# A dilated convolution with a gate: one more family of products split into shared and private parts, and the gate's product moved from VectorE to GpSimd

## The chip, the cores and the metric

The kernel runs on one core of a Trainium2 chip. The metric is the device time of one execution in microseconds (us). PE is TensorE (PEld its weight loads), DVE is VectorE, ACT is ScalarE, POOL is GpSimd, SP is SyncE, which here only issues DMAs.

## The reference

```python
B, T, D, K = 2, 16000, 144, 15          # x: (B,T,D), w: (K,D,2D), w_o: (D,D), all bfloat16
dil = 2; pad = (K - 1) * dil
xp = jnp.pad(x, ((0, 0), (pad, 0), (0, 0)))
h = sum(einsum('btc,cd->btd', xp[:, pad - i*dil : pad - i*dil + T, :], w[i]) for i in range(K))
z = tanh(h[..., :D]) * sigmoid(h[..., D:])
return z @ w_o
```

It is a causal convolution in time with 15 taps and dilation 2 from 144 to 288 channels, a gate (tanh of one half times sigmoid of the other), and a 144 x 144 projection.

## The kernel before, in words

**Tiling.** Time is cut into 16 windows of 2048 steps (8 for each of the two sequences). A window is loaded transposed (`xn`: 128 channels on partitions, time along the free dimension). The other 16 channels go another way: `xt` is gathered, ACT and DVE turn it into two signals `xs` (steps `cr` and `dr`), these are written to a DRAM buffer `xg` (`wg`) and come back transposed as `rx` and `re`, in which 8 taps x 16 channels fill the 128 partitions. A window has two octets, one for each parity `rho` of time, since the dilation is 2; there are 32 octets. An octet is 128 x 8 outputs of 288 channels: partition m and phase r stand for time 16 m + 2 r + rho. The output of a phase is accumulated in a PSUM bank of 128 x 288 fp32.

**Fewer products.** The 15 taps (and a zero one, `w_all`) are applied by a nested fast scheme: DVE forms differences of the signal in time (`d2`, `d4`, `d8`, `d24`, `d28`, `d48`, `d248`: the name lists the shifts), sums of taps are formed once, and sums that several outputs share are computed once. The class `Leaf` is a product with a shared and two private parts: `common` (two matmuls into a first bank; step `v`), `copy` (ACT copies that bank into a second one; step `k`), `private(i)` (two matmuls into bank i, and a third on `rx` or `re` where the leaf has a remainder; step `p`). `dup` (step `d`) has ACT copy a bank once more. The leaves are A1, A2, A3 (two banks of the pool `ps_a`) and B1, C1, E1 (five banks of the pool `ps_bc`). A method `direct` adds products with single taps into a bank without sharing: B2 and B3 for the even phases, C2 for the odd ones (five matmuls each, for i = 0 and 1).

**From banks to outputs.** ACT copies A1 to SBUF (`a1s`). DVE forms q2 = a1s - A2 and q3 = a1s + A3, and from them and the banks the fp32 outputs `y[:, k + 4 i, :]`: yB2 (k = 0), yC2 (k = 1), yB3 (k = 2), yC3 (k = 3). For yC3 a `t3` = q3 + C1 comes first and E1 is added; for yC2 the C1 bank holds C1 and C2 together. Gate 0 (k = 0 and 2, steps `th0`, `sg0`) and gate 1 (k = 1 and 3, `th1`, `sg1`) are each one tanh and one sigmoid of 576 elements on ACT; `m0` and `m1` are their products z, on DVE. A DMA transposes z (`zt`), eleven matmuls in three groups project it (`g0` to `g2`), ACT casts the result (`po0` to `po2`), and the second octet of a window stores it (`ost`).

**Order.** All engines are scheduled by hand: an engine runs its instructions in program order, and waits on other engines by semaphores; buffers of a pool are given out in rotation. The program order comes from the list `PLAN`: each entry `name:at` says that octet n's step is issued in period n + at, at its place in the list. The list is cyclic: one pass is one period, that is one octet's worth of every engine's work. Steps that belong to a window (the loads, the remainder, the differences) are issued for even n alone. The list `first` issues the beginning of octet 0, and `finish_early` and `finish` the end: the last octet's z is transposed on PE, and the last three octets are projected there.

Of the kernel before, what the change touches and what calls it, by code (L numbers as in the profile page):

```python
# [26 lines left out]
def kernel(  # L27
# [14 lines left out]
    nc = tc.nc  # L42
# [88 lines left out]
    pad = {"x": 0, "d8": 0}  # L131

    def derive_steps(s):
        ahead = {"x": 0}

        def sub(name, of, d, first=None, run=0):
# [4 lines left out]
            def go(which=slice(None)):  # L141
# [15 lines left out]
                for form in forms[which]:  # L157
# [6 lines left out]
                    d28=sub("d28", "d2", 8, 6, 4), d24=sub("d24", "d2", 4, 2, 4), d248=sub("d248", "d24", 8, 8, 2))  # L164
# [97 lines left out]
    ev = wtile(2, "ev")  # L262
# [82 lines left out]
    class Octet:  # L345
        by_phase = False

        def __init__(self, s, rho):
            self.s, self.rho = s, rho
            self.A1 = Leaf(s, True, "x", "d8", rho, lambda j: a1v[:, j, :], lambda j, i: ss[:, 2 * j + i, :])  # L350
            self.A2 = Leaf(s, s is not sets[0] or rho > 0, "d4", "d48", rho - 4, lambda j: av[:, j, 1, :], lambda j, i: quad[:, j, i, 1, :],
                           ("rx", rho, ns_r[:]))
            self.A3 = Leaf(s, True, "d4", "d48", rho, lambda j: av[:, j, 0, :], lambda j, i: quad[:, j, i, 0, :],
                           ("rx", rho + 4, s_r[:]))
            self.B1, self.C1 = (Leaf(s, False, "d2", "d28", rho - 2 * e, lambda j, e=e: bcv[:, j, e, :],
                                     lambda j, i, e=e: bc[:, 2 * j + i, e, :]) for e in (1, 0))
            self.E1 = Leaf(s, False, "d24", "d248", rho, lambda j: ev[:, j, :], lambda j, i: w_all[:, 8 * j + 4 * i, :], ("re", rho + 4, we_r[:]))
            self.g, self.t, self.po = {}, {}, {}

        def get(self, pool, name, shape, dt):  # L360
            if name not in self.t:
                self.t[name] = pool.tile(shape, dt, name=name)
            return self.t[name]
# [19 lines left out]
        def C2(self, i):  # L383
            self.direct(self.C1.ts[i], self.rho - 4 + 8 * i, lambda j: w_all[:, 4 * j + 2, :], 4, "re", self.rho + 8 * i, we_r[:])

        def t3(self, i):
            nc.vector.tensor_tensor(out=self.get(cp_pool, "t3", [P, 2, D2], F32)[:, i, :], in0=self.t["q3"][:, i, :],  # L387
                                    in1=self.C1.ts[i][:, 0:D2], op=ALU.add)

        def out_y(self, k, ts, q, op, i):  # L390
            y = self.get(y_pool, "y", [P, 8, D2], F32)
            nc.vector.tensor_tensor(out=y[:, k + 4 * i, :], in0=self.t[q][:, i, :], in1=ts[i][:, 0:D2], op=op)  # L392

        def act(self, k, name, lo, func):
            t = act_pool.tile([P, 4, D], BF16, name=name)
            self.g[name, k] = t
            nc.scalar.activation(out=t[:], in_=self.t["y"][:, k::2, lo:lo + D], func=func)  # L397

        def mult(self, k, part):
            z = self.get(z_pool, "z", [P, 9, CM], BF16)  # L400
            o, lo, n = dict(a=(z[:, k:8:2, :], 0, CM), b=(z[:, 8, :].rearrange("p (r c) -> p r c", c=CR)[:, k::2, :], CM, CR),
                            z=(z[:].rearrange("p g c -> p (g c)").rearrange("p (r c) -> p r c", c=D)[:, k::2, :], 0, D))[part]
            th, sg = self.g["th", k], self.g["sg", k]
            nc.vector.tensor_tensor(out=o, in0=th[:, :, lo:lo + n], in1=sg[:, :, lo:lo + n], op=ALU.mult)  # L404
# [6 lines left out]
    def z_by_pe(o, blocks, by):  # L411

        zt, z = o.get(zt_pool, "zt", [P, 9, P], BF16), o.t["z"]
        for i in range(0, len(blocks), 4):
            b = blocks[i:i + 4]
            ps = bank(True)[:].bitcast(BF16).rearrange("p (g m) -> p g m", m=256)
            for k, g in enumerate(b):
                nc.tensor.transpose(ps[:, k, 0:P], z[:, g, :], ident[:])
            copy_by(by, zt[:, b[0]:b[-1] + 1:2, :], ps[:, 0:len(b), 0:P])
        o.zt = zt  # L420
# [7 lines left out]
    def outproj(o, g, end=False):  # L428
        r0, n = 3 * g, min(3, 8 - 3 * g)
        o.po[g] = bank(False) if end else ps_o.tile([P, 512], F32, name="po", tag="po")  # L430
        if not o.by_phase:
            for c in range(r0, r0 + n + 1):
                a, e = max(c - 1, r0), min(c + 1, r0 + n)
                nc.tensor.matmul(o.po[g][:, (a - r0) * D:(e - r0) * D], lhsT=o.zt[:, c, :],  # L434
                                 rhs=wo_z[:, c, a - c + 1:e - c + 1, :].rearrange("p r e -> p (r e)"), start=c == r0, stop=c == r0 + n,
                                 skip_group_check=True)
            return
        nc.tensor.matmul(o.po[g][:, 0:n * D], lhsT=o.zt[:, 8, :], rhs=wo_bd[:, r0:r0 + n, :].rearrange("p r e -> p (r e)"),  # L438
                         start=True, stop=False)
        for i in range(n):  # L440
            nc.tensor.matmul(o.po[g][:, i * D:(i + 1) * D], lhsT=o.zt[:, r0 + i, :], rhs=wo_m[:], start=False, stop=i == n - 1)  # L441
# [16 lines left out]
    def issue(n, name):  # L458
# [16 lines left out]
        if name[0] in "vkpd" and name[1] in "ABCE":  # L475
# [7 lines left out]
        elif name[:2] == "t3":  # L483
            o.t3(int(name[-1]))
        elif name[:3] == "a1s":
            o.a1s(int(name[-1]))
        elif name[0] == "q":
            o.q(*((o.A2, "q2") if name[1] == "2" else (o.A3, "q3")), int(name[-1]),
                ALU.subtract if name[1] == "2" else ALU.add)
        elif name[0] in "BC":  # L490
            getattr(o, name[0:2])(int(name[-1]))
        elif name[0] == "y":
            leaf = {"B": o.B1, "C": o.C1, "E": o.E1}["E" if name[1:3] == "C3" else name[1]]
            ts, q = (leaf.other, "q3") if name[1:3] == "B3" else (leaf.ts, "t3" if name[1:3] == "C3" else "q2")
            k = (0 if name[1] == "B" else 1) + (2 if name[2] == "3" else 0)
            o.out_y(k, ts, q, ALU.subtract if name[1] == "B" else ALU.add, int(name[-1]))
        elif name[:2] == "th":
            o.act(int(name[2]), "th", 0, ACT.Tanh)
        elif name[:2] == "sg":
            o.act(int(name[2]), "sg", D, ACT.Sigmoid)  # L500
        elif name[0] == "m":
            for part in "ab" if o.by_phase else "z":
                o.mult(int(name[1]), part)
        elif name == "zt":
            o.zt = z_load(o.t["z"])
# [14 lines left out]
    def finish_early():  # L520

        n = NO - 3
        for g in range(3):
            outproj(live[n], g, g > 0)
        for g, by in ((0, "DVE"), (1, "DVE"), (2, "ACT")):
            project_out(live[n], window_out(n), g, by)
        z_by_pe(live[NO - 1], [0, 2, 4, 6], "ACT")

    def finish():
        n = NO - 2  # L530
        store(NW - 2, nc.sync)
# [17 lines left out]
    at_wg = next((at, i) for i, (name, at) in enumerate(plan) if name == "wg")  # L549
    def weights_out():  # L550
# [4 lines left out]
        nc.gpsimd.tensor_copy(out=held[:], in_=ev[0:1, 0, 0:1])  # L555
# [9 lines left out]
    def evs():  # L565
        add(ev[:], w_all[:, 0:16:8, :], w_all[:, 4:16:8, :])
        weights_out()
# [9 lines left out]
    done = [(0, f) for f in first if not callable(f)] + late2 + [(0, "d24"), (0, "d248")]  # L577
    todo = sorted((2 + at_wg[0], False, at_wg[1] - .5, n, name) if n == 2 and name in ("cr", "dr") else
                  (n + at, n > 1 and n + at < 0, i, n, name) for i, (name, at) in enumerate(plan) for n in range(NO)
                  if not (name in even and (n % 2 or n == 0) or name == "ost" and n % 2 == 0  # L580
                          or name in outwards and n >= NO - 3 or name == "zt" and n == NO - 1))
    gates = [(NO - 1, "m1")]
    for *_, n, name in todo:
        if (n, name) in done:
            continue
        if (n, name) in gates:
            gates.clear()
            finish_early()
        issue(n, name)
    finish()  # L590
# [28 lines left out]
```

## Time and profile before

| what | value |
|---|---|
| time, median of 3 runs | 332.19 us (331.83 to 332.69) |
| the profiled execution: its own time | 332.82 us |
| its span, instructions | 330.8 us, 7432 |
| PE busy, matmuls | 321.4 us (97%), 2657 |
| DVE busy, instructions | 293.5 us (89%), 664 |
| ACT busy, instructions | 242.0 us (73%), 571 |
| POOL busy, instructions | 26.3 us (8%), 56 |
| granted TensorE clock, mean | 0.999 |

The profile is of one execution, so numbers from it are made against 332.82 us; 2.0 us of that lie outside the span. A duration is from an instruction's start to its end; instructions of one engine overlap a little, so that the distance of two starts is what an instruction takes from its engine. Matmuls are pipelined: a busy PE isn't PE at its peak, and for them too the distance of starts counts. After an arrow the profile names who ended the idle time before an instruction.

### The profile page before, as it was taken

How to read it: one execution, taken by the hardware profiler on the slowest of the kernel's cores; microseconds unless marked ns; L12 is line 12 of the kernel's file. 1: busy time of each engine (PE TensorE's matmuls, PEld its weight loads, DVE VectorE, ACT ScalarE, POOL GpSimd, SP SyncE). 2: the span in 40 equal slices, each digit the busy share in tenths (PEclk: the TensorE clock that was granted, in tenths of full speed). 3: DMA queues.
4: the chain of work that ended last, by engine and by line, in shares of the span. 5: the costliest groups of instructions: out<-in, count | busy, mean ns of one | idle time of the engine just before them, and what ended most of it. 6: DMA issues, size and time to landing. Idle time of an engine off the chain costs nothing.

```text
span 330.8 us, 7432 instructions
## 1 busy us (share of the span) xinstructions
PE 321.4 (97%) x2657; PEld 303.1 (92%) x2657; DVE 293.5 (89%) x664; ACT 242.0 (73%) x571; POOL 26.3 (8%) x56
## 2 busy tenths in 40 slices
PE   8899999999999999999999999999999999999993
PEld 3589999999999999999999999999999999999982
DVE  2889999989999998999999899999989999998683
ACT  2737777777877777788777778877777787777763
POOL 5959100000000000000000000000000000000000
PEclk9999999999999999999999999999999999999999
DMA  8779897895949579594979769495986859594113
GB/s 173 160 139 157 155 210 138 151 185 100 206 109 204 151 130 222 77 213 102 175 181 169 157 119 187 109 209 137 145 208 119 171 112 189 154 143 132 38 36 129
DMA packets 194993, 49.64 MB, mean 150 GB/s; under 512 B 190487, under 2 KB 192896, under 8 KB 194957
## 3 DMA queue, kind: packets, MB, share of 16 engines
q1 hardware_dynamic: 188894, 40.07, 69.6%
q10 hardware_dynamic: 4799, 8.58, 7.0%
q0 software_dynamic: 1264, 0.53, 0.9%
q8 instruction: 20, 0.33, 0.4%
q14 instruction: 16, 0.13, 0.1%
HBM read 2.82 MB, written 11.40 MB: 43 GB/s over the span
## 4 chain that ended last, share of the span: by engine, by line
PE 90%; DMA 4%; SPq 2%; DVE 2%; issue 1%; POOL 1%; ACT 0%; DVEq 0%
PE bc L302 56%; PE a L302 25%; PE po L434 9%; DMA xn<-in_x_dram 2%; DMA xt<-in_x_dram 1%; SPq L128 1%; DMA xg<-zero 1%; SPq L89 1%; DVE d L160 0%; DVE o L426 0%; DVE y L392 0%; DVE z L404 0%; POOL xg L123 0%; PE bc L438 0%; PE bc L441 0%
## 5 line engine op out<-in xcount | busy, mean ns | idle before, releaser
L302 PEld LDWEIGHTS <-d 128*128 128x128 bf16 x1792 | 225.4, 145 | 7.8 <-issue 1.4
L302 PE MATMUL bc<-w_all,d 128*128 128x288 bf16 x832 | 140.0, 286 | 0.3 <-DVE t L387 0.3
L392 DVE TENSOR_TENSOR y<-q,bc 128x288 f32<-128x288 f32 x192 | 86.4, 450 | 7.6 <-PE bc L302 5.7
L331 ACT COPY bc<-bc 128x288 f32<-128x288 f32 x97 | 38.5, 397 | 30.1 <-PE bc L302 24.3
L369 DVE TENSOR_TENSOR q<-a1s,a 128x288 f32<-128x288 f32 x126 | 54.2, 451 | 1.5 <-PE a L302 0.8
L424 ACT CAST o<-po 128x432 bf16<-128x432 f32 (+1 forms) x87 | 41.7, 479 | 17.1 <-PE po L434 17.1
L160 DVE TENSOR_TENSOR d<-d 128x516 bf16<-128x516 bf16 (+3 forms) x65 | 52.2, 805 | 0.0
L302 PE MATMUL a<-sm,d 128*128 128x288 bf16 x252 | 50.2, 286 | 0.0
L331 ACT COPY a<-a 128x288 f32<-128x288 f32 x95 | 36.6, 386 | 13.6 <-PE a L302 10.6
L160 DVE TENSOR_TENSOR d<-xn 128x516 bf16<-128x516 bf16 (+2 forms) x48 | 41.1, 859 | 5.1 <-DMA xn<-in_x_dram 5.1
L397 ACT ACTIVATE th<-y 128x576 bf16<-128x576 f32 x64 | 43.9, 685 | 1.1 <-DVE y L392 1.1
L397 ACT ACTIVATE sg<-y 128x576 bf16<-128x576 f32 x64 | 43.7, 683 | 0.0
L434 PE MATMUL po<-wo_z,zt 128*128 128x144 bf16 (+1 forms) x323 | 43.4, 253 | 0.0
L302 PE MATMUL bc<-bc,d 128*128 128x288 bf16 x256 | 41.8, 286 | 0.0
L302 PE MATMUL bc<-wo_p,re 128*128 128x288 bf16 x128 | 36.6, 286 | 0.0
L302 PE MATMUL bc<-we_r,re 128*128 128x288 bf16 x128 | 36.6, 286 | 0.0
L387 DVE TENSOR_TENSOR t<-q,bc 128x288 f32<-128x288 f32 x64 | 28.8, 451 | 8.3 <-PE bc L302 8.3
L434 PEld LDWEIGHTS <-zt 128*128 128x128 bf16 x341 | 29.9, 98 | 4.1
L335 ACT COPY bc<-bc 128x288 f32<-128x288 f32 x64 | 25.0, 393 | 11.2 <-PE bc L302 7.0
L392 DVE TENSOR_TENSOR y<-t,bc 128x288 f32<-128x288 f32 x64 | 26.1, 450 | 5.9 <-PE bc L302 5.9
L404 DVE TENSOR_TENSOR z<-th,sg 128x576 bf16<-128x576 bf16 (+1 forms) x66 | 29.1, 443 | 0.0
L302 PEld LDWEIGHTS <-re 128*128 128x128 bf16 x256 | 28.8, 113 | 0.0
(79 smaller groups left out, 275.5 us busy)
## 6 DMA issues: line engine op xcount, KB each, us to landing
out_dram<-o ACTq DMA_DIRECT2D x13, 576.0 KB
xg<-xs SPq DMA_DIRECT2D x30, 65.0 KB
xt<-in_x_dram SPq DMA_DIRECT2D x13, 71.5 KB
w_all<-in_w_dram SPq DMA_DIRECT2D x3, 288.0 KB
out_dram<-o SPq DMA_DIRECT2D x1, 576.0 KB
zt<-z SPq DMA_TRANSPOSE x31
out_dram<-o ACTq DMA_DIRECT2D x1, 468.0 KB
out_dram<-o ACTq DMA_DIRECT2D x1, 288.0 KB
```

The source lines that it names most:

```text
L89: nc.sync.dma_start_transpose(out=xn[:, lo:WB], in_=src)
L160: nc.vector.tensor_tensor(out=o, in0=a, in1=b_, op=ALU.subtract)
L302: nc.tensor.matmul(ps[:, 0:D2], lhsT=l, rhs=r, start=start, stop=stop, skip_group_check=on)
L331: nc.scalar.copy(out=self.ts[1][:, 0:D2], in_=self.ts[0][:, 0:D2])
L335: nc.scalar.copy(out=self.other[i][:, 0:D2], in_=self.ts[i][:, 0:D2])
L369: nc.vector.tensor_tensor(out=self.get(cp_pool, name, [P, 2, D2], F32)[:, i, :], in0=self.t["a1s"][:, i, :], in1=leaf.ts[i][:, 0:D2], op=op)
L387: nc.vector.tensor_tensor(out=self.get(cp_pool, "t3", [P, 2, D2], F32)[:, i, :], in0=self.t["q3"][:, i, :], in1=self.C1.ts[i][:, 0:D2], op ...
L392: nc.vector.tensor_tensor(out=y[:, k + 4 * i, :], in0=self.t[q][:, i, :], in1=ts[i][:, 0:D2], op=op)
L397: nc.scalar.activation(out=t[:], in_=self.t["y"][:, k::2, lo:lo + D], func=func)
L404: nc.vector.tensor_tensor(out=o, in0=th[:, :, lo:lo + n], in1=sg[:, :, lo:lo + n], op=ALU.mult)
L424: nc.scalar.copy(out=o, in_=a)
L434: nc.tensor.matmul(o.po[g][:, (a - r0) * D:(e - r0) * D], lhsT=o.zt[:, c, :], rhs=wo_z[:, c, a - c + 1:e - c + 1, :].rearrange("p r e -> p ...
```

## The change

- C2 is no longer a direct product. A leaf F1 takes its place, like E1, on `d24` and `d248`, with a remainder: a common part (`vF`), a copy on ACT (`kF`) and two private parts (`pF_0`, `pF_1`), in two banks of its own. `ev` holds the sums of taps for E1 and F1, and `d248` is formed for three times as many elements (runs of 6 of 16 instead of 2).
- q2 and q3 are the halves of one tile `q`. `t` is formed for both in one instruction of 576 elements, the C1 bank being read twice; yC2 is then t + F1, and yC3 is t + E1.
- z (`m0`, `m1`) is formed on GpSimd for octets 2 to 30, on DVE for octets 0, 1 and 31.
- `PLAN` is another list. In `first`, octet 2's `cr`, `dr` and `wg` (window 1) are issued at the end, and its gather `xt` goes ahead of its load `xl`.
- At the end, gate 1 of the last octet is done in halves (y[1], y[5], then y[3], y[7], as `act(1, 4)` and `act(3, 4)`); where `PLAN` comes to `th1` and `sg1` of the last octet, these two are issued. `finish` takes over `finish_early`'s work in another order, the transposes on PE go by the halves, and `outproj_last` projects by the order in which blocks arrive.

The diff, cut to its core:

```diff
 PLAN = """
-    zt:3 m0:2 d24:0 pA1_0:0 g0:3 pA1_1:0 pC_0:1 pC_1:1 a1s_0:0 d2:-1 rx:0 vA2:0 po0:3 wg:-1 yB2_1:1
-    a1s_1:0 m1:2 t3_0:1 vE:1 d4:-1 g1:3 kA2:0 yB3_0:1 t3_1:1 C2_0:1 yB3_1:1 po1:3 re:0 kE:1 pA2_0:0
-    d28:0 q2_0:0 g2:3 pA2_1:0 C2_1:1 yC2_0:1 po2:3 vB:0 q2_1:0 ost:3 d8:-1 vA3:0 pE_0:1 kB:0 pE_1:1
-    d248:0 yC2_1:1 pB_0:0 kA3:0 pB_1:0 d48:-1 yC3_1:1 pA3_0:0 cr:-2 dB_0:0 th0:1 yC3_0:1 q3_0:0 pA3_1:0
-    sg0:1 dB_1:0 B2_0:0 B3_0:0 th1:1 vC:0 q3_1:0 vA1:-1 B3_1:0 kA1:-1 sg1:1 B2_1:0 xl:-2 dr:-2 yB2_0:0
-    xt:-3 kC:0
+    q3_1:0 cr:-2 q3_0:0 zt:2 g2:3 rx:-1 m0:1 po2:3 yB2_0:0 B2_1:0 yB2_1:0 dr:-2 d4:-1 d8:-2 xt:-4 vA1:-1
+    vC:0 B3_0:0 kA1:-1 pA1_0:-1 ost:3 kC:0 d28:-1 B3_1:0 a1s_0:-1 th1:1 pA1_1:-1 vF:0 a1s_1:-1 d48:-1
+    pC_0:0 pC_1:0 vA2:-1 yB3_0:0 d248:0 g0:2 yB3_1:0 kF:0 m1:1 kA2:-1 t_0:0 vE:0 kE:0 t_1:0 pF_0:0
+    pA2_0:-1 yC2_0:0 th0:0 pA2_1:-1 sg0:0 pF_1:0 vB:-1 q2_0:-1 q2_1:-1 kB:-1 pE_0:0 pE_1:0 vA3:-1
+    pB_0:-1 po0:2 yC2_1:0 yC3_0:0 d24:-1 re:-1 g1:2 pB_1:-1 kA3:-1 d2:-2 pA3_1:-1 pA3_0:-1 yC3_1:0
+    dB_0:-1 xl:-3 B2_0:-1 po1:2 wg:-2 dB_1:-1 sg1:0
 """
...
-    pad = {"x": 0, "d8": 0}
+    pad = {"x": 0, "d8": 0, "d248": 0}
...
-                    d28=sub("d28", "d2", 8, 6, 4), d24=sub("d24", "d2", 4, 2, 4), d248=sub("d248", "d24", 8, 8, 2))
+                    d28=sub("d28", "d2", 8, 6, 4), d24=sub("d24", "d2", 4, 2, 4), d248=sub("d248", "d24", 8, 4, 6))
...
-            self.E1 = Leaf(s, False, "d24", "d248", rho, lambda j: ev[:, j, :], lambda j, i: w_all[:, 8 * j + 4 * i, :], ("re", rho + 4, we_r[:]))
+            self.E1, self.F1 = (Leaf(s, False, "d24", "d248", rho - 4 * e, lambda j, e=e: ev[:, j, e, :],
+                                     lambda j, i, e=e: w_all[:, 8 * j + 4 * i + 2 * e, :], ("re", rho + 4 - 4 * e, we_r[:])) for e in (0, 1))
...
-        def C2(self, i):
-            self.direct(self.C1.ts[i], self.rho - 4 + 8 * i, lambda j: w_all[:, 4 * j + 2, :], 4, "re", self.rho + 8 * i, we_r[:])
-
-        def t3(self, i):
-            nc.vector.tensor_tensor(out=self.get(cp_pool, "t3", [P, 2, D2], F32)[:, i, :], in0=self.t["q3"][:, i, :],
-                                    in1=self.C1.ts[i][:, 0:D2], op=ALU.add)
+        def t(self, i):
+            ps = self.C1.ts[i][:, 0:D2]
+            nc.vector.tensor_tensor(out=self.get(cp_pool, "t", [P, 2, 2, D2], F32)[:, :, i, :], in0=self.b["q"][:, :, i, :],
+                                    in1=bass.AP(ps.tensor, ps.offset, [ps.ap[0], [0, 2], [1, D2]]), op=ALU.add)
...
+        def act(self, k, step=2):
+
+            for name, lo, func in (("th", 0, ACT.Tanh), ("sg", D, ACT.Sigmoid)):
+                self.gate(k, name, lo, func, step)
+
+        def gate(self, k, name, lo, func, step=2):
+            t = self.g[name, k] = act_pool.tile([P, 8 // step, D], BF16, name=name + "h" * (step == 4))
+            nc.scalar.activation(out=t[:], in_=self.b["y"][:, k::step, lo:lo + D], func=func)
...
         elif name[0] == "m":
-            for part in "ab" if o.by_phase else "z":
-                o.mult(int(name[1]), part)
+            o.mult(int(name[1]), eng=nc.gpsimd if 2 <= n < NO - 1 else nc.vector)
...
+        a, b, c = (live[n] for n in range(NO - 3, NO))
+        c.at = {}
+        window_out(NO - 1)
         for g in range(3):
-            outproj(live[n], g, g > 0)
...
+            outproj(a, g, g > 0)
+        outproj(b, 0, True)
+        z_by_pe(c, [0, 2, 4, 6], "ACT")
+        c.mult(1, 4)
+        c.mult(3, 4)
...
+        z_by_pe(c, [1, 5], "ACT")
+        z_by_pe(c, [3, 7, 8], "DVE")
...
-        add(ev[:], w_all[:, 0:16:8, :], w_all[:, 4:16:8, :])
+        four = w_all[:].rearrange("p (j i e o) d -> p j i e o d", i=2, e=2, o=2)
+        add(ev[:], four[:, :, 0, :, 0], four[:, :, 1, :, 0])
...
-             "q3_0", "pA3_1", "B2_0", "q3_1", "B2_1", evs, "yB2_0", pre0["d248"]]
-    late2 = [(2, "xl")]
+             "q3_0", "pA3_1", "B2_0", "q3_1", "B2_1", evs, "yB2_0", pre0["d248"], *(lambda k=k: issue(2, k) for k in "cr dr wg".split())]
+    late2 = [(2, "xt"), (2, "xl")]
...
+    last = {"th1": lambda: live[NO - 1].act(1, 4), "sg1": lambda: live[NO - 1].act(3, 4), "m1": finish}
```

More of the change, by code (lines that the diff above doesn't have):

```diff
@@ L400, in mult @@
+        def mult(self, k, step=2, eng=nc.vector):
             z = self.get(z_pool, "z", [P, 9, CM], BF16)
-            o, lo, n = dict(a=(z[:, k:8:2, :], 0, CM), b=(z[:, 8, :].rearrange("p (r c) -> p r c", c=CR)[:, k::2, :], CM, CR),
-                            z=(z[:].rearrange("p g c -> p (g c)").rearrange("p (r c) -> p r c", c=D)[:, k::2, :], 0, D))[part]
             th, sg = self.g["th", k], self.g["sg", k]
-            nc.vector.tensor_tensor(out=o, in0=th[:, :, lo:lo + n], in1=sg[:, :, lo:lo + n], op=ALU.mult)
+            if not self.by_phase:
+                parts = [(z[:].rearrange("p g c -> p (g c)").rearrange("p (r c) -> p r c", c=D)[:, k::step, :], 0, D)]
+            else:
+                parts = [(z[:, k:8:step, :], 0, CM), (z[:, 8, :].rearrange("p (r c) -> p r c", c=CR)[:, k::step, :], CM, CR)]
+            for o, lo, n in parts:
+                eng.tensor_tensor(out=o, in0=th[:, :, lo:lo + n], in1=sg[:, :, lo:lo + n], op=ALU.mult)
@@ L411, in z_by_pe @@
     def z_by_pe(o, blocks, by):
[L413 to L420, printed above, removed]
+        zt, z = o.get(zt_pool, "zt", [P, 9, P], BF16), o.b["z"]
+        ps = bank(True)[:].bitcast(BF16).rearrange("p (g m) -> p g m", m=256)
+        n = len(o.at)
+        for k, g in enumerate(blocks):
+            o.at[g] = n + k
+            nc.tensor.transpose(ps[:, k, 0:P], z[:, g, :], ident[:])
+        copy_by(by, zt[:, n:n + len(blocks), :], ps[:, 0:len(blocks), 0:P])
     def copy_by(by, o, a):
@@ L430, in outproj, with outproj_last @@
         o.po[g] = bank(False) if end else ps_o.tile([P, 512], F32, name="po", tag="po")
[L431 to L441, printed above, removed]
+        for c in range(r0, r0 + n + 1):
+            a, e = max(c - 1, r0), min(c + 1, r0 + n)
+            nc.tensor.matmul(o.po[g][:, (a - r0) * D:(e - r0) * D], lhsT=o.zt[:, c, :],
+                             rhs=wo_z[:, c, a - c + 1:e - c + 1, :].rearrange("p r e -> p (r e)"), start=c == r0, stop=c == r0 + n,
+                             skip_group_check=True)
+    def outproj_last(o, blocks):
+        for c in blocks:
+            g, lo, n, w_ = (c // 3, c % 3, 1, wo_m[:]) if c < 8 else \
+                (c - 8, 0, min(3, 8 - 3 * (c - 8)), wo_bd[:, 3 * c - 24:min(3 * c - 21, 8), :].rearrange("p r e -> p (r e)"))
+            new = g not in o.po
+            if new:
+                o.po[g] = bank(False) if g else ps_o.tile([P, 512], F32, name="po", tag="po")
+            nc.tensor.matmul(o.po[g][:, lo * D:(lo + n) * D], lhsT=o.b["zt"][:, o.at[min(c, 8)], :], rhs=w_, start=new, stop=c >= 8,
+                             skip_group_check=True)
     def project_out(o, ob, g, by="ACT"):
@@ L474, in issue @@
         o = live[n]
-        if name[0] in "vkpd" and name[1] in "ABCE":
+        if name[0] in "vkpd" and name[1] in "ABCEF":
             leaf = getattr(o, name[1:3] if name[1] == "A" else name[1] + "1")
@@ L487, in issue @@
         elif name[0] == "q":
[L488 to L490 removed]
+            o.q(*((o.A2, 0) if name[1] == "2" else (o.A3, 1)), int(name[-1]), ALU.subtract if name[1] == "2" else ALU.add)
+        elif name[0] == "B":
             getattr(o, name[0:2])(int(name[-1]))
         elif name[0] == "y":
[L493 to L494 removed]
+            leaf = {"B": o.B1, "C2": o.F1, "C3": o.E1}[name[1] if name[1] == "B" else name[1:3]]
+            ts, q = (leaf.other if name[1:3] == "B3" else leaf.ts), "q" if name[1] == "B" else "t"
             k = (0 if name[1] == "B" else 1) + (2 if name[2] == "3" else 0)
@@ L554, in weights_out @@
         held = const.tile([1, 1], BF16)
-        nc.gpsimd.tensor_copy(out=held[:], in_=ev[0:1, 0, 0:1])
+        nc.gpsimd.tensor_copy(out=held[:], in_=ev[0:1, 0, 0, 0:1])
         for g in range(9):
@@ L576 @@
         f() if callable(f) else issue(0, f)
-    done = [(0, f) for f in first if not callable(f)] + late2 + [(0, "d24"), (0, "d248")]
-    todo = sorted((2 + at_wg[0], False, at_wg[1] - .5, n, name) if n == 2 and name in ("cr", "dr") else
-                  (n + at, n > 1 and n + at < 0, i, n, name) for i, (name, at) in enumerate(plan) for n in range(NO)
+    done = [(0, f) for f in first if not callable(f)] + late2 + [(0, "d24"), (0, "d248")] + [(2, k) for k in "cr dr wg".split()]
+    todo = sorted((n + at, n > 1 and n + at < 0, i, n, name) for i, (name, at) in enumerate(plan) for n in range(NO)
                   if not (name in even and (n % 2 or n == 0) or name == "ost" and n % 2 == 0
                           or name in outwards and n >= NO - 3 or name == "zt" and n == NO - 1))
-    gates = [(NO - 1, "m1")]
+    last = {"th1": lambda: live[NO - 1].act(1, 4), "sg1": lambda: live[NO - 1].act(3, 4), "m1": finish}
     for *_, n, name in todo:
@@ L585 @@
             continue
[L586 to L590, printed above, removed]
+        if n == NO - 1 and name in last:
+            last[name]()
+        else:
+            issue(n, name)
 _INS = ['x', 'w', 'w_o']
```

60 lines of the change are left out of this document (23 added, 37 removed).

## The prediction

> **What bounds the kernel now.** I read the page first (busy shares and the chain of work that ended last), then busy times by stretch for two periods in the middle, then the timelines of PE, DVE and ACT over those periods, then the groups by shape for prices.
>
> ```profile
> span 330.8 us, 7432 instructions
> ...
> PE 321.4 (97%) x2657; PEld 303.1 (92%) x2657; DVE 293.5 (89%) x664; ACT 242.0 (73%) x571; POOL 26.3 (8%) x56
> ...
> PE 90%; DMA 4%; SPq 2%; DVE 2%; issue 1%; POOL 1%; ACT 0%; DVEq 0%
> ```
> ```profile
> 200.05:209.63 9.58, 9.58 (x84) 9.28 (x82) 8.73 (x20) 7.61 (x20) 0.00 (x0) 1.00 0.91 188
> 209.63:219.21 9.58, 9.58 (x84) 9.27 (x82) 9.16 (x22) 7.24 (x19) 0.00 (x0) 1.00 0.85 121
> ```
> The chain is PE for 90%, and in the stretches (length, then busy time of PE, PEld, DVE, ACT, POOL, then clock) PE is busy for all of each 9.58 us period at a granted clock of 1.00. One period is one octet. The timeline gives what a matmul really takes:
>
> ```profile
> 156.91 0.66 PE L302 MATMUL bc<-w_all,d 128*128 128x288 bf16 x4
> 157.41 0.29 PE L302 MATMUL bc<-we_r,re 128*128 128x288 bf16 x1
> 157.53 0.41 PE L302 MATMUL a<-sm,d 128*128 128x288 bf16 x2
> ```
> These five are C2_0: 157.53 - 156.91 = 0.62 us, so about 0.123 us each from start to start; the 0.286 us of the groups is pipelined. An octet has 70 of these (8.58 us) and 11 output matmuls (0.37 + 0.37 + 0.24 = 0.98 us): 9.56 us, the period. So a matmul less is 0.123 us less, until another loop is longer than PE's.
>
> **PE.** C2 (2 x 5 matmuls) goes; leaf F1 comes (common 2, private 2 x 3). Ten become eight: 2 x 0.1225 = 0.245 us per octet, a period of 9.33 us, and 32 x 0.245 = 7.85 us in all.
>
> **DVE.** Durations overlap, so I price by distance of starts.
>
> ```profile
> 157.35 0.45 DVE L387 TENSOR_TENSOR t<-q,bc 128x288 f32<-128x288 f32 x1
> 157.71 0.45 DVE L392 TENSOR_TENSOR y<-q,bc 128x288 f32<-128x288 f32 x1
> ...
> 160.14 0.68 DVE L160 TENSOR_TENSOR d<-d 128x1032 bf16<-128x1032 bf16 x1
> 160.74 0.81 DVE L392 TENSOR_TENSOR y<-t,bc 128x288 f32<-128x288 f32 x2
> ```
> ```profile
> L160 DVE TENSOR_TENSOR d<-d 128x1032 bf16<-128x1032 bf16 x32 | 22.0, 688 | 0.0
> L160 DVE TENSOR_TENSOR d<-d 128x2072 bf16<-128x2072 bf16 x15 | 18.5, 1233 | 0.0
> L160 DVE TENSOR_TENSOR d<-d 128x516 bf16<-128x516 bf16 x16 | 10.4, 650 | 0.0
> L404 DVE TENSOR_TENSOR z<-th,sg 128x576 bf16<-128x576 bf16 x62 | 28.0, 452 | 0.0
> ```
> An fp32 288-wide one costs 0.367 us, a 1032-wide bf16 difference 0.60; everywhere the distance is the duration less 0.08. Per window (two octets) before: 28 x 0.367 for q, t, y, 4 x 0.37 for z, 0.23 for xs, 5.07 for the seven differences: 17.06 us of 19.15. After: z leaves (-1.48); each of four t's doubles to 576 fp32 elements, 288 more at one per cycle, 0.30 us (+1.20); d248 grows from 516 to 1548 elements. 1032 and 2072 elements give 0.524 ns per element, so 0.96 us against 0.65 (+0.31); if the runs of 6 go at the rate of the 516 row (runs of 2), up to +1.3. I take +0.31, the neighbouring runs of 4 being on the fast line. Sum 17.1 us (up to 18.1) of 18.66 available: DVE is fuller (92%) but not the bound by its sum.
>
> **ACT.** kF adds a copy of 0.30 us per octet: about 7.3 of 9.33 us. Only its place in the order matters (below).
>
> **z on GpSimd.** The trace has no such product on POOL; the nearest rows:
>
> ```profile
> L552 POOL MEMSET wo_z<- 128x2592 bf16 x1 | 2.3, 2278 | 0.0
> L553 POOL MEMSET wo_bd<- 128x1152 bf16 x1 | 1.1, 1077 | 0.0
> L220 POOL TENSOR_SCALAR_AFFINE_SELECT swap<-swap 128x128 bf16<-128x128 bf16 x1 | 0.3, 333 | 0.1
> ```
> Two memsets give 0.834 ns per element and 0.116 us fixed: 0.60 us for 576 written elements, the lower end. The select (the two in the trace, 333 and 292 ns, average 312) has one input: (312 - 116) / 128 = 1.53 ns per element, 1.00 us for 576. A second input stream at memset rate makes 1.48 us; both inputs at the select's rate, 1.88, the upper end. I take 1.25, midway between one input and the cheaper second. POOL has nothing else by then but two or three memsets of 0.12 us; its weight DMAs end at 35 us, the first z there is due at about 45.
>
> By the Trainium skill, "GPSIMD Engine Reference", section "Performance versus the Vector engine", a two-input add of 2048 fp32 elements takes 4497 ns on GpSimd; scaled to 576 that is an estimate of 1.26 us. No run here shows it yet, and the sum would be the same by it.
>
> **Where each z falls: a walk of one period.** PE's new order, by 0.1225 us a matmul from g2 at 0, puts vA1 at 0.73, B3_0 1.22, pA1_0 1.83, vF 2.94, g0 3.92, vE 4.29, pF_0 4.53, vB 6.00, pE_0 6.25, g1 7.48 and B2_0 at 8.83. A copy follows its matmul's end by 0.03 us, and ACT's distances are
>
> ```profile
> 160.80 0.38 ACT L335 COPY bc<-bc 128x288 f32<-128x288 f32 x1 [0.54 <-PE bc L302]
> 161.09 0.69 ACT L397 ACTIVATE th<-y 128x576 bf16<-128x576 f32 x1
> 161.68 0.68 ACT L397 ACTIVATE sg<-y 128x576 bf16<-128x576 f32 x1
> 162.25 0.40 ACT L335 COPY bc<-bc 128x288 f32<-128x288 f32 x1
> ```
> so kE starts at 4.73, th0 5.03, sg0 5.62 and ends at 6.30. m0 is alone on POOL and starts at about 6.37 whatever its place in the list: until 7.62. th1 ends at 3.32, so m1 runs from about 3.4 to 4.6. DVE's differences lie at 1.3 to 3.3 (dr, d8, d248 in even periods, d4, d28, d48 in odd ones) and, as d24 or d2 (1.15 us), from 7.0. m1 meets none of them; m0 lies under the start of d24 or d2.
>
> PSUM: ten tenancies share the five bc banks instead of eight, and each is given back by a DVE read. By the walk kE's bank (from t_0) comes free 0.1 us ahead in odd periods, vE's 0.4, kC's 0.8, the rest more. The A banks: vA1 needs q3_0's read. Cost zero while DVE keeps this pace; the cover is 0.1 us at kE, and a t_0 later by more moves th0, sg0 and m0 with it. SP: zt, rx, re and xl take 9.6 us of issue in odd periods, zt, xt and wg 3.9 in even ones; m1 ends at 4.6 of the period ahead of the one that reads zt, and g0 stands at 3.92 of that: hidden by some 6 us, even where zt queues behind xl.
>
> **Ends.** Head: xt of window 1 now goes ahead of xl, and DVE's 0.86 us wait at 22 us, behind which PE waited 0.66, should go; the wider ev and d248 take back 0.2: -0.4. z of octets 0 and 1 stays on DVE, two full periods: +0.2. Tail: the plan has sg1 a period ahead of th1, so the half gates of y[3], y[7] are issued ahead of those of y[1], y[5], all four after the last y: four at 0.33 instead of two at 0.59, and four z pieces instead of two: +0.3; the split transposes give back 0.1.
>
> **Sum.** The profiled execution took 332.82 us (span 330.8), 0.63 above the median of 332.19. 332.82 - 7.85 - 0.4 + 0.2 + 0.2 = 324.97 for it, 324.3 for the median. For the thin covers I add 0.03 us in each of 29 periods: 325.2.
>
> **Rival 1: d24 and d2 wait for m0.** If a DVE instruction with two SBUF inputs can't run beside a z, d24 (or d2) starts at m0's end: 7.62 + 1.15, yC3_1 and q3_1 0.73, q3_0 0.45, 0.04 to PE: 9.99, against vA1 due at 10.06. At 1.25 us that only eats slack; the period is 9.33 + (z - 1.32). At 1.48 it is 9.49, +4.6 us: 329. For: the loop has 0.07 us of cover. Against: no row of before shows DVE held by POOL (POOL's few reads there met no two-input difference). The Trainium skill, "SBUF — State Buffer", section "Who interferes with whom", states just this, for the whole instruction; the 115 ns after a release of its section "A bandwidth-pool intuition that's wrong (but worth ruling out)" would be an estimate of about +0.05 us per period here, 326.
>
> **Rival 2: slower, the same loop with a slow z.** From z = 1.32 + 0.245 = 1.57 us the held loop is longer than today's 9.575. At the upper end of 1.88 us the period is 9.89: +0.32 x 29 = 9 us, 341. For: two strided inputs per element on an engine whose only measured read costs 1.53 ns. Against: it needs both the hold and a rate beyond the second stream's.
>
> **Rival 3: DVE or the banks.** With d248 on the slow line, or t_0 0.3 us late every period, kE, th0, sg0 and m0 move and PE waits about 0.2 us at vA1 or vE: the gain is nearly eaten, 330 to 333.
>
> **Chances.** Forecast (324 to 326.3) 0.54; rival 1 and smaller waits (326.3 to 331) 0.21; rival 3 0.06, most of it within 0.3% (1.0 us, about what a measurement of this kernel can tell from no change); rival 2 and anything slower 0.17; below 324, from the ends, 0.02. Faster 0.78, same 0.04, slower 0.18. The range leaves out most of rival 2 and a little below: 323.4 to 333.2.
>
> **What would show it.** Right: periods of 9.33 with 79 matmuls and no PE wait on a DVE read; t at 0.75, d248 at 0.96, z on POOL at 1.0 to 1.5. Rival 1: d24 and d2 well above 1.23 us, or idle before them that ends with POOL, and PE waiting on q (L369). Rival 2: POOL's z near 1.9 us. Rival 3: d248 at 1.6 us, or ACT's kE waiting for DVE's t. The forecast is wrong if the period is above 9.40.

## The result, and the profile after

| | before | changed |
|---|---|---|
| time, median of 4 runs | 332.44 us (331.83 to 332.96) | 327.74 us (327.41 to 328.66) |
| ratio, 95% interval | | 0.986 (0.984 to 0.988) |
| the profiled execution, its span | 332.82, 330.8 us | 328.66, 326.9 us |

The changed kernel is 4.7 us faster by the medians, where 7.0 were forecast, and its time lies 2.5 us above the forecast of 325.2 (before's median has moved by 0.25 us with its fourth run). The page of the profile after:

```profile
span 326.9 us, 7432 instructions
...
PE 316.1 (97%) x2593; PEld 294.5 (90%) x2593; DVE 304.2 (93%) x607; ACT 250.9 (77%) x606; POOL 100.9 (31%) x114
...
PE 83%; DMA 6%; DVE 4%; issue 2%; SPq 1%; POOL 1%; ACT 1%; POOLq 0%; DVEq 0%
```
64 matmuls fewer, as drawn up; but PE's part of the chain of work fell from 90% to 83%, and DMA's and DVE's rose from 4 and 2 to 6 and 4. The chain leaves PE at the two ends and, in the middle, at one place of note (a difference on DVE at 281 us; below). Busy times by stretch, two periods in the middle (columns as before):

```profile
204.91:214.32 9.41, 9.41 (x82) 8.95 (x80) 9.21 (x19) 7.87 (x20) 2.57 (x2) 1.00 0.87 118
214.32:223.65 9.33, 9.33 (x82) 9.02 (x80) 9.24 (x19) 7.52 (x19) 2.57 (x2) 1.00 1.15 204
```
The period is 9.33 and 9.42 in turn instead of 9.58 throughout, with two exceptions among the longer ones: one is 9.38, one 9.60. PE counts as busy for all of the 9.41, since the 0.286 us of a matmul's record cover more than the 0.123 us from start to start; the lost 0.09 us doesn't show in these sums, but in the waits of PEld below. The groups by shape (behind the bars: busy us in all, mean ns of one; then the idle time before them, and what ended it):

```profile
L410 POOL TENSOR_TENSOR z<-th,sg 128x576 bf16<-128x576 bf16 x58 | 74.5, 1285 | 206.3 <-ACT th L400 143.6 <-issue 35.9 <-ACT sg L400 23.2
...
L386 DVE TENSOR_TENSOR t<-q,bc 128x576 f32<-128x576 f32 x64 | 45.1, 746 | 0.0
...
L160 DVE TENSOR_TENSOR d<-xn 128x2078 bf16<-128x2078 bf16 x16 | 25.1, 1566 | 0.0
L160 DVE TENSOR_TENSOR d<-d 128x2072 bf16<-128x2072 bf16 x15 | 24.0, 1601 | 0.0
...
L160 DVE TENSOR_TENSOR d<-d 128x1548 bf16<-128x1548 bf16 x16 | 15.6, 976 | 0.0
```
z on GpSimd takes 1.285 us, a t 0.746 and d248 0.976. But d2 (2078 elements) and d24 (2072) went from 1.24 and 1.23 to 1.57 and 1.60 us: the mark that rival 1 named. In the timeline of one period:

```profile
205.54 1.28 POOL L410 TENSOR_TENSOR z<-th,sg 128x576 bf16<-128x576 bf16 x1 [1.79 <-issue]
```
```profile
206.30 1.61 DVE L160 TENSOR_TENSOR d<-d 128x2072 bf16<-128x2072 bf16 x1
```
z ends at 206.82, d24 at 207.91, 1.09 us later: its record begins 0.52 us ahead of z's end, but all except 0.14 us of the 1.23 that it takes alone came after that. From 60 to 302 us, every d24 and d2 ends 1.09 or 1.10 us behind a z. PE's B2_0 needs d24 next; the waits of PEld for it sum to 2.2 us in 11 instances, such as

```profile
301.86 0.33 PEld L302 LDWEIGHTS <-d 128*128 128x128 bf16 x3 [0.16 <-DVE d L160]
```
The longest, 0.34 us at 283 us, is the period of 9.60: z started later there, and d24, held for longer (1.79 us), ended later.

At the head, PE and DVE from their timelines:

```profile
24.18 0.62 DVE L160 TENSOR_TENSOR d<-xn 128x516 bf16<-128x516 bf16 x1 [2.14 <-DMA xn<-in_x_dram]
```
```profile
25.49 0.41 PE L302 MATMUL bc<-ev,d 128*128 128x288 bf16 x2 [2.26 <-DVE y L391]
...
34.53 0.41 PE L302 MATMUL bc<-ev,d 128*128 128x288 bf16 x2 [0.41 <-DVE y L391]
```
DVE waits 2.14 us for window 1's xn, whose DMA the chain shows from 16.94 for 7.21 us; y and, through the banks, PE wait behind it. Before, PE lost 0.66 us at this place. In a second profile of the changed kernel ("changed again" below) DVE's wait is 1.72 us, and PE's too.

Three numbers place the time in every run below: the start of octet 5's first A1 matmul (head), the distance of those starts from octet to octet (period), and from octet 31's to the end of the span (tail). A1 stands elsewhere in the new order, so before's head and tail shift a little against the others. Times are medians; head, period and tail are of the profiled execution. In the kernels with 9.42 or 9.36 in the table one period, from octet 28 to 29, is 9.58 to 9.61.

| kernel | time, us | head | period | tail |
|---|---|---|---|---|
| before | 332.44 | 57.58 | 9.58 | 24.2 |
| changed (first profile) | 327.74 | 59.31 | 9.33 / 9.42 | 23.7 |
| changed again | 327.46 | 58.21 | 9.33 / 9.42 | 23.8 |
| z on VectorE | 325.82 | 57.90 | 9.33 | 23.7 |
| m0 on VectorE | 326.26 | 58.16 | 9.33 | 23.8 |
| xl ahead of xt | 328.35 | 60.02 | 9.33 / 9.42 | 23.8 |
| both loads early | 326.80 | 57.17 | 9.33 / 9.42 | 23.7 |
| z on VectorE, loads early, half gates in order | 324.49 | 57.12 | 9.33 | 23.2 |
| m0 twice on GpSimd | 326.97 | 58.00 | 9.33 / 9.36 | 23.7 |
| memsets for z | 325.86 | 57.75 | 9.33 | 23.9 |
| B2_0 later | 326.34 | 57.58 | 9.33 / 9.34 | 23.7 |
| two matmuls more | 333.69 | 58.14 | 9.57 | 23.9 |
| as the 324.49 us one, but m1 of octets 0 to 29 on GpSimd | 324.89 | 57.43 | 9.33 | 23.2 |

### The profile page after: what moved, and what is told of

Its sections match the earlier page's. It is cut to its first block, busy times and chain, and to the rows that moved or that the text cites. A ratio compares the mean times of both kernels' runs of the same rounds, so it can differ in the third digit from the quotient of the medians.

```text
span 326.9 us, 7432 instructions
## 1 busy us (share of the span) xinstructions
PE 316.1 (97%) x2593; PEld 294.5 (90%) x2593; DVE 304.2 (93%) x607; ACT 250.9 (77%) x606; POOL 100.9 (31%) x114
## 4 chain that ended last, share of the span: by engine, by line
PE 83%; DMA 6%; DVE 4%; issue 2%; SPq 1%; POOL 1%; ACT 1%; POOLq 0%; DVEq 0%
PE bc L302 51%; PE a L302 24%; PE po L438 9%; DMA xn<-in_x_dram 4%; DVE d L160 2%; DVE y L391 1%; DMA zt<-z 1%; SPq L128 1%; DMA xg<-zero 1%; POOLq L620 0%; POOL z L410 0%; DVE q L370 0%; ACT zt L429 0%; ACT o L429 0%; POOL xg L123 0%
## 5 line engine op out<-in xcount | busy, mean ns | idle before, releaser
L302 PEld LDWEIGHTS <-d 128*128 128x128 bf16 x1728 | 215.9, 145 | 12.0 <-issue 3.5
L410 POOL TENSOR_TENSOR z<-th,sg 128x576 bf16<-128x576 bf16 x58 | 74.5, 1285 | 206.3 <-ACT th L400 143.6
L302 PE MATMUL bc<-w_all,d 128*128 128x288 bf16 x704 | 127.6, 287 | 0.2
L331 ACT COPY bc<-bc 128x288 f32<-128x288 f32 x129 | 50.1, 388 | 19.7 <-PE bc L302 10.9
L160 DVE TENSOR_TENSOR d<-d 128x1032 bf16<-128x1032 bf16 (+2 forms) x65 | 61.8, 972 | 0.0
L391 DVE TENSOR_TENSOR y<-t,bc 128x288 f32<-128x288 f32 x128 | 56.7, 448 | 2.8
L391 DVE TENSOR_TENSOR y<-q,bc 128x288 f32<-128x288 f32 x128 | 55.8, 448 | 3.0 <-PE bc L302 1.5
L160 DVE TENSOR_TENSOR d<-xn 128x516 bf16<-128x516 bf16 (+2 forms) x48 | 46.5, 972 | 7.6 <-DMA xn<-in_x_dram 7.6
L386 DVE TENSOR_TENSOR t<-q,bc 128x576 f32<-128x576 f32 x64 | 45.1, 746 | 0.0
L367 ACT COPY a1s<-a 128x288 f32<-128x288 f32 x64 | 25.4, 398 | 10.2 <-PE a L302 10.1
```

The source lines that it names most:

```text
L160: nc.vector.tensor_tensor(out=o, in0=a, in1=b_, op=ALU.subtract)
L302: nc.tensor.matmul(ps[:, 0:D2], lhsT=l, rhs=r, start=start, stop=stop, skip_group_check=on)
L331: nc.scalar.copy(out=self.ts[1][:, 0:D2], in_=self.ts[0][:, 0:D2])
L367: nc.scalar.copy(out=self.get(cp_pool, "a1s", [P, 2, D2], F32)[:, i, :], in_=self.A1.ts[i][:, 0:D2])
L386: nc.vector.tensor_tensor(out=self.get(cp_pool, "t", [P, 2, 2, D2], F32)[:, :, i, :], in0=self.b["q"][:, :, i, :], in1=bass.AP(ps.tensor, ...
L391: nc.vector.tensor_tensor(out=y[:, k + 4 * i, :], in0=self.b[name][:, k // 2, i, :], in1=ts[i][:, 0:D2], op=op)
```

## The experiments

**z back on VectorE** (of the changed kernel, as are all below unless said):

```diff
-            o.mult(int(name[1]), eng=nc.gpsimd if 2 <= n < NO - 1 else nc.vector)
+            o.mult(int(name[1]))
```


> The changed kernel with every z back on VectorE, in the same order; GpSimd is then empty after the head. Hold theory (d24 and d2 can't run beside a z on GpSimd): d24 and d2 return from 1.60 and 1.57 us to 1.23. DVE then carries 17.1 + 1.48 = 18.6 us per window of 18.66, so it is full and PE waits on it: a period of 9.4 to 9.7 us, 329 to 337 us. Rival (the move was not needed): the period stays at 9.33, 326 to 327 us.

325.82 us, ratio 0.983 (0.981 to 0.985), 1.9 us under the changed kernel by the medians. Groups by shape:

```profile
L160 DVE TENSOR_TENSOR d<-xn 128x2078 bf16<-128x2078 bf16 x16 | 19.8, 1237 | 0.0
L160 DVE TENSOR_TENSOR d<-d 128x2072 bf16<-128x2072 bf16 x15 | 18.4, 1227 | 0.0
```
The differences are back at 1.23 us, and every period is 9.32 or 9.33. The second part of the hold theory's expectation fell: with 18.6 us of work in 18.65 DVE still keeps PE's pace. So the move to GpSimd took nothing off the path, and it cost 0.09 us per window: 26 periods take 242.46 us here and 243.85 in the changed kernel. The other 0.5 us between the medians are less than the head differs by between two profiles of the changed kernel itself (59.31 and 58.21).

**m0 alone back on VectorE.**

```diff
+            o.mult(int(name[1]), eng=nc.gpsimd if name == "m1" and 2 <= n < NO - 1 else nc.vector)
```


> The changed kernel with gate 0's z (m0) on VectorE and gate 1's (m1) left on GpSimd. Hold theory: m0 was what d24 and d2 waited for, m1 meets no difference; d24 and d2 return to 1.23 us, DVE's extra 0.37 us goes into the 0.6 us that the hold took, and every period is 9.33 us instead of 9.33 and 9.42 in turn: 13 to 14 x 0.09 = 1.2 us less, about 326.5. Rival (DVE is simply full, the longer d24 is not a hold): 0.74 us more DVE work per window makes the period longer, 9.5 and up, 330 or more.

326.26 us, ratio 0.984 (0.982 to 0.986); d24 and d2 at 1.230 and 1.234 us, every period 9.325. m1, still on GpSimd at 1.283 us, costs nothing, because it falls where no difference runs. It was m0 alone, as the hold theory said, and DVE wasn't simply full.

**Something on GpSimd that only writes.** z of octets 2 to 30 is left out.

```diff
+            if eng is nc.gpsimd:
+                o = parts[0][0]
+                eng.tensor_copy(out=o[0:1, 0, 0:1], in_=(sg if k == 0 else th)[0:1, 0, 0:1])
+                for _ in range(2):
+                    eng.memset(o, 0.0)
+                return
```


> The changed kernel with each z on GpSimd replaced by a one-element copy from the same gate (so that it starts at the same time) and two memsets of z's size, which write SBUF and read nothing; the product of octets 2 to 30 is left out. About as long on GpSimd (0.2 + 2 x 0.6 us). Rule that only a reading GpSimd instruction holds a DVE instruction with two SBUF inputs: d24 and d2 go back to 1.23 us and every period is 9.33 us, about 326.5. Rival (anything on GpSimd holds it): d24 and d2 stay at 1.5 us and more, and the periods alternate between 9.33 and 9.42.

```profile
L413 POOL MEMSET z<- 128x576 bf16 x116 | 67.0, 578 | 6.8
...
L160 DVE TENSOR_TENSOR d<-xn 128x2078 bf16<-128x2078 bf16 x16 | 19.7, 1234 | 0.0
L160 DVE TENSOR_TENSOR d<-d 128x2072 bf16<-128x2072 bf16 x15 | 18.4, 1230 | 0.0
```
GpSimd is as busy in the same places (0.18 + 2 x 0.58 us), and d24 and d2 are free, every period 9.325. So being busy and writing don't hold a difference; what is left out is the reading of two inputs (and the multiplication). The Trainium skill's "SBUF — State Buffer", section "Who interferes with whom", says so (DVE instructions with two SBUF inputs contend with a GpSimd instruction that reads SBUF, not with one that only writes), and the trace agrees on both sides: 1.60 us beside z, 1.23 beside memsets.

**m0 twice on GpSimd.**

```diff
+            for _ in range(2 if name == "m0" and 2 <= n < NO - 1 else 1):
                 o.mult(int(name[1]), eng=nc.gpsimd if 2 <= n < NO - 1 else nc.vector)
```


> The changed kernel with gate 0's z formed twice on GpSimd, one after the other: 1.28 us more there in every period, nothing more anywhere else. Hold theory: d24 and d2 last up to 1.28 us longer (2.9 us as recorded), since they end 1.1 us behind the second z; the thin covers are used up, and the period grows by 1.1 to 1.29 us: 32 to 37 us in all, about 362. Rival (GpSimd beside DVE costs nothing, or only a share of a rate): d24 and d2 stay near 1.6 us or grow by less than half of 1.28, the time by less than 15 us.

326.97 us: my expectation was off by 35 us, and the rival's "stays near 1.6 us" came out, but not for its reason. The timelines of GpSimd and DVE:

```profile
203.81 3.53 POOL L410 TENSOR_TENSOR z<-th,sg 128x576 bf16<-128x576 bf16 x2 [1.75 <-ACT sg L400]
```
```profile
204.63 1.55 DVE L160 TENSOR_TENSOR d<-d 128x2072 bf16<-128x2072 bf16 x1
```
The two z together take 3.53 us instead of 2.57; the second of a pair 2.16 instead of 1.28. The first z ends at 205.09; d24, on record since 204.63, goes next and ends at 206.18, 1.09 us later; the second z, on record since 205.17, ends at 207.34, 1.16 us behind d24. So the two engines take turns, each for a whole instruction, and d24 waited for one z only. That is a hold, and the second z of the pair paid its price on an engine that nobody waits for. The first z also starts 0.05 us sooner here after sg0's end (0.08 us instead of 0.14), d24 is 0.04 us shorter, and the long period is 9.36 instead of 9.42: as far as these two kernels show it, the period follows d24's end.

**Where the hold is paid.**

```diff
-    q3_1:0 cr:-2 q3_0:0 zt:2 g2:3 rx:-1 m0:1 po2:3 yB2_0:0 B2_1:0 yB2_1:0 dr:-2 d4:-1 d8:-2 xt:-4 vA1:-1
+    q3_1:0 cr:-2 q3_0:0 zt:2 g2:3 B2_0:0 rx:-1 m0:1 po2:3 yB2_0:0 B2_1:0 yB2_1:0 dr:-2 d4:-1 d8:-2 xt:-4 vA1:-1
...
-    dB_0:-1 xl:-3 B2_0:-1 po1:2 wg:-2 dB_1:-1 sg1:0
+    dB_0:-1 xl:-3 po1:2 wg:-2 dB_1:-1 sg1:0
```


> The changed kernel with B2_0 one place later on PE, behind g2 instead of ahead of it (0.24 us), z on GpSimd as it is. If the hold is paid where PE's B2_0 waits for d24, that wait of 0.1 us in every other period goes, though d24 and d2 stay at 1.6 us: all periods 9.33, about 1.2 us less than the changed kernel, 326.3. Rival (the hold is paid through q3_0 and vA1, as the prediction had it): the periods keep alternating with 9.42.

326.34 us, ratio 0.983 (0.982 to 0.985). d24 and d2 stay at 1.598 and 1.563 us, and the longest period is 9.34:

```profile
L160 DVE TENSOR_TENSOR d<-d 128x2072 bf16<-128x2072 bf16 x15 | 24.0, 1598 | 0.0
```
The waits of PEld for d24, 11 in the changed kernel, are gone (after 57 us none is longer than 0.03 us), and 26 periods take 242.62 us, 0.16 more than with z on VectorE. With z on GpSimd and everything held as before, 0.24 us of slack at B2_0 takes the loss away. So it was paid at B2_0's need for d24, not at vA1.

**The price of a matmul.** z on VectorE, and two matmuls more per octet, adding zeros:

```diff
+            if name == "g0":
+                for _ in range(2):
+                    nc.tensor.matmul(o.po[0][:, 0:D2], lhsT=zero[:, 0:P], rhs=zero[:, 0:D2], start=False, stop=True, skip_group_check=True)
```


> The changed kernel with every z on VectorE (uniform periods of 9.325 us) and two matmuls of 288 columns more per octet, which add zeros behind g0, so that the number of matmuls is that of before. PE theory: the period is 9.325 + 0.245 = 9.57 us, before's own, and the time about 7.6 us above 325.8: 333. Rival (DVE, 18.6 of 18.66 us per window, is what sets 9.325): the added work fits beside it in part, the period stays below 9.5.

The period is 9.57 us, before's own within 0.01; 333.69 us in one run, 2.8 of them outside the span (1.8 to 2.1 in the other profiles), so that the period is the better measure. It grew by all of what two matmuls cost, 0.245 us: with z on VectorE it is PE's own sum that sets 9.325, though in that kernel DVE has no gap between its records from 100 to 250 us.

**The head: the order of the two loads.**

```diff
-    late2 = [(2, "xt"), (2, "xl")]
+    late2 = [(2, "xl"), (2, "xt")]
```


> The changed kernel with window 1's load xl ahead of its gather xt again, as before the change. If the order on SP's queue delayed xn: it lands near 20.7 us instead of 24.15, DVE's wait of 2.14 us and PE's of 2.26 go, and PE waits 0.7 us for the gather instead, as before: 1.3 to 1.6 us less, about 326.3. Rival (xn was late from other traffic, or by chance): xn still lands after 23 us and the time stays at 327.7.

328.35 us, ratio 0.990 (0.988 to 0.993), if anything slower. xn is in time now, but the loss only moved. ACT, from its timeline, and PE:

```profile
21.74 0.46 ACT L113 COPY xs<-xt 104x320 bf16<-104x320 bf16 x1 [3.77 <-DMA xt<-in_x_dram]
22.11 0.39 ACT L331 COPY a<-a 128x288 f32<-128x288 f32 x1
```
```profile
22.55 0.41 PE L302 MATMUL a<-ss,d 128*128 128x288 bf16 x2 [2.16 <-ACT a L331]
```
`first` now issues `cr` where the copy kA1 stands right behind it on ACT's queue, so a late gather stops A1, and PE for 2.16 us. Whichever load comes second is late; my expectation took the wait for the gather from before (0.7 us) without looking at what is queued behind `cr` in the new order.

**Both loads ahead of rx and re.**

```diff
+    gather(1)
+    sets[1].update(load(1))
     remainder(0, 0)
     remainder(0, 1)
...
-    for n, name in late2:
-        issue(n, name)
+    sets[1].update(steps=derive_steps(sets[1]))
```


> The changed kernel with both loads of window 1 issued ahead of rx and re of window 0 on SP's queue, where SP waits 4 us for the buffer in DRAM. Queue theory: xn and xt land before 17 us, DVE and PE wait for neither: 2.2 to 2.6 us less, about 325.3. Rival (the loads then delay what the first octet needs): rx and re land later by up to 2 us, PE waits there instead, 327 to 328.

The wait for xn is gone from both engines: d8, in its timeline,

```profile
21.99 0.66 DVE L160 TENSOR_TENSOR d<-xn 128x516 bf16<-128x516 bf16 x1
```
starts without one, and octet 5 begins 2.1 or 1.0 us earlier than in the two profiles of the changed kernel. The time, 326.80 us, is 0.7 to 0.9 below theirs, but the ratios (0.986 against 0.986 and 0.984) don't tell them apart: the changed kernel's own runs spread from 325.69 to 328.66 us, and this one's from 326.48 to 326.99. The rival of the expectation came true in part as well: rx lands later, and PE waits 0.97 us for it (0.36 and 0.18 in the two profiles of the changed kernel):

```profile
16.70 0.31 PE L304 MATMUL bc<-ns_r,rx 128*128 128x288 bf16 x1 [0.97 <-DMA rx<-xg]
```
The rest of the head's loss is put down to DVE, by stretch of an octet from octet 1 to 4:

```profile
19.86:28.63 8.77, 8.69 (x70) 8.27 (x69) 8.77 (x20) 5.74 (x14) 7.98 (x16) 1.00 0.75 118
28.63:38.10 9.47, 9.02 (x71) 8.23 (x69) 9.47 (x22) 6.34 (x17) 5.11 (x11) 1.00 1.13 169
38.10:47.60 9.50, 9.48 (x82) 9.00 (x80) 9.50 (x20) 7.28 (x18) 1.28 (x1) 1.00 0.59 119
```
DVE (the third busy time) has no gap at all; the second of these has no output matmuls yet and should take PE 9.33 - 0.98 = 8.35 us. The last experiment tests this.

**A version that beats both.** z on VectorE, both loads early, and the last octet's half gates in the order in which their y come (the third edit alone is shown):

```diff
-    last = {"th1": lambda: live[NO - 1].act(1, 4), "sg1": lambda: live[NO - 1].act(3, 4), "m1": finish}
+    last = {"sg1": lambda: live[NO - 1].act(1, 4), "th1": lambda: live[NO - 1].act(3, 4), "m1": finish}
```


> The changed kernel with every z on VectorE, both loads of window 1 ahead of rx and re, and the last octet's half gates of y[1], y[5] ahead of those of y[3], y[7]. If the three costs are separate they add up against the changed kernel: -1.2 us (no d24 waits for GpSimd), -2.1 (no wait for xn in the head; as much of it as DVE, busy all the time until 57 us, lets through), -0.2 in the tail: 324 to 325 us. Rival (the head's loss is DVE's, not the load's): z on VectorE brings nothing more there and the sum is 325.5 or more.

324.49 us, ratio 0.977 (0.975 to 0.980); beside it on the same chip the changed kernel:

> The changed kernel itself, beside the others on this chip: the yardstick for them, about 327.7 us and 0.986 of before.

327.46 us, ratio 0.984 (0.981 to 0.987). 3.0 us lie between the two medians, and 3.1 between the spans of their profiles: 1.1 in the head, 1.4 in the 26 periods (243.85 against 242.46 us) and 0.6 in the tail. The sum was met with parts that were not: 2.1, 1.2 and 0.2 were expected. ACT at the end, first of the changed kernel (its first profile), then of this one:

```profile
317.55 0.44 ACT L400 ACTIVATE thh<-y 128x288 bf16<-128x288 f32 x1 [0.51 <-DVE y L391]
...
318.56 0.43 ACT L400 ACTIVATE sgh<-y 128x288 bf16<-128x288 f32 x1
```
```profile
313.61 0.43 ACT L402 ACTIVATE thh<-y 128x288 bf16<-128x288 f32 x1
...
314.61 0.43 ACT L402 ACTIVATE sgh<-y 128x288 bf16<-128x288 f32 x1
```
In the changed kernel all four follow the last y (it waits 0.51 us for it); from that y's end at 317.52 the last gate needs 1.47 us. In order, the last y ends at 314.19 and the last gate 0.85 us later. The tail has another wait that no run here tests: PEld waits for the zt of the last z that goes by DMA, 1.0 us in the changed kernel and 0.5 with z on VectorE; before had none there.

**Less on DVE in the head.** The same with m1 of octets 0 to 29 on GpSimd:

```diff
-            o.mult(int(name[1]))
+            o.mult(int(name[1]), eng=nc.gpsimd if name == "m1" and n < NO - 2 else nc.vector)
```


> The kernel with z on VectorE, early loads and the half gates in order (324.5 us), with gate 1's z (m1) on GpSimd for octets 0 to 29, where it meets no difference. If VectorE, busy without a break up to 57 us, is what costs the head 1.4 us, two z less on it there give 0.4 to 0.7 us: about 323.9, with periods of 9.325 as before. Rival (octet 0's z, behind GpSimd's weight DMAs until 36 us, comes too late for its projection): PE waits for zt at 41 us, 325 or more.

324.89 us, ratio 0.979 (0.978 to 0.980): no gain. Before the first z on GpSimd, octet 1 had already begun 0.46 us later in this profile than in that of the 324.49 us kernel, with rx 0.2 us later. From octet 1 to octet 5 it took 37.01 us against 37.16, so what DVE was spared brought 0.15 us. The trace shows where the rest of the gain went. The z that GpSimd had from 35.27 to 36.57 us met d24, which started at 36.02 and took 1.65 us, not 1.23; octet 3 came 9.58 us after octet 2 (9.47 there). The second, at 41.38, met d248, which had started first: this time z was held and took 1.62 us, and d248 its usual 0.97. From octet 3 on the periods are 9.33 (9.52 and 9.41 there), so DVE does set the pace of these early octets, and m1 meets differences in them after all.

## Why the prediction was right, and where its sum was off

**The time.** 327.74 us is inside the range that was given (323.4 to 333.2), but above the forecast's own band (324 to 326.3, chance 0.54); it lies in that of rival 1 and smaller waits (326.3 to 331, chance 0.21). What put it there is in part the hold (1.4 us in 26 periods, 0.9 of them allowed for), and more the two ends (1.7 us).

**The gain: right.** Two matmuls of 0.1225 us fewer per octet; a floor of 9.33 us, shown with z on VectorE (9.325) and taken back by two added matmuls (9.57).

**The prices: right.** z on GpSimd 1.285 us (taken: 1.25), t 0.746 (0.75), d248 0.976 (0.96, so the runs of 6 are on the fast line). That a distance of starts is everywhere the duration less 0.08 isn't so: d248 of before lasted 0.65 us and took 0.48 from start to start, so it grew by 0.40, not 0.31. The sum of 17.1 us per window holds all the same (18.54 with z on VectorE, less 1.47 for z). The estimate of 1.26 us, scaled from a figure of the Trainium skill's "GPSIMD Engine Reference", section "Performance versus the Vector engine", agrees as well.

**Rival 1: the hold came true, its loop didn't.** d24 and d2 do wait for m0, and the walk placed that overlap, with m0's end some 0.6 us behind the start of d24 (0.52 measured). The loop was the wrong one. It closed through yC3_1, q3 and vA1 with 0.07 us to spare; the walk never listed that B2_0, at 8.83, reads d24 in the very period in which d24 is formed. (B2_0 has four matmuls, three of them on d24; B3's and C2's are five.) By rival 1's own numbers a held d24 ended at 7.62 + 1.15 = 8.77, with next to no cover. Hence 0.09 us in every second period, 0.05 on average. That 0.03 was allowed for in the sum, for other waits, and that rival 1 had about 0.05 by another path, is luck: neither counted this reader. Of the signs that were named, the mean period is 9.38, below the 9.40 that would have been wrong, though every second one is above it; "no PE wait on a DVE read" failed. The price of another 115 ns after a release, which the Trainium skill's "SBUF — State Buffer" gives in its section "A bandwidth-pool intuition that's wrong (but worth ruling out)", for descriptors that GpSimd writes behind a VectorE copy, doesn't show here: d24 ended 1.09 us after z, less than its own 1.23.

**DVE's fullness: harmless in the middle, as said, and more so.** Even at 18.6 us of work per window it didn't set the period, so giving it back 1.48 us by GpSimd bought nothing in the middle. The prediction costed the move and never asked what the period would be without it.

**The ends are the mis-sized term.** 26 periods took 5.17 us less than before, 0.199 each; over 32 octets that would be 6.4 us, where the sum had 7.85 - 0.87 = 7.0. The medians differ by 4.7, so by this estimate the ends cost 1.7 us, where the sum had -0.4 + 0.2 + 0.2 = 0. The step that failed is "xt of window 1 now goes ahead of xl, and DVE's 0.86 us wait should go: -0.4". That wait did go, but xn, now second, landed at 24.15 us, and DVE waited 2.14 us for it. The prediction counted the place that xt won on SP's queue, not the one that xl lost; nor did it see that a DVE at 92% takes long to catch up on a delay: after this wait it has no gap until 59.5 us. In the run that puts both loads early the wait is gone, and 0.7 to 0.9 us of time with it, which the noise of the head doesn't set apart. The tail was forecast at +0.2; from the end of the last y to the end of the span it went from 8.95 to 9.36 us, +0.4, for the reason given there (the half gates in the wrong order): with them in order, the tail is 0.5 us shorter than with z on VectorE alone.

## What to carry to other kernels

Before work is moved off an engine, ask what the period is with the work left there: an engine that is 99% full and not on the path, as DVE was here, needs no relief, and the helper that takes the work can hold up what it was to relieve. When a queue is put in a new order, price both what moves up and what moves down, with everything that stands behind the waiting instruction; and follow each late result to all its readers, the nearest in time first.

## What the runs showed of the hardware that was not expected

The product on GpSimd, which reads SBUF, and a DVE difference with two SBUF inputs exclude each other for a whole instruction, whichever starts first (d24 took 1.65 us behind z, z 1.62 behind d248), but take turns: of two z in a row the second let the waiting d24 through and took 2.16 us instead of 1.28. And DVE stayed on PE's pace, 9.325 us per octet, without a gap between its records from 100 to 250 us; the shortest distances of starts add up to 18.54 us per window of 18.65, an estimate that leaves 0.1 us to spare.
